# Wider VectorE operations, a 16-bit softmax and a re-cut start in a fused attention and GEGLU block on one Trainium2 core

## The chip, the cores and the metric

The kernel runs on one core of one Trainium2 chip. The metric is the device time of one execution in microseconds; a kernel's time is the median of several runs. Beside the runs there is one profiled execution, whose trace gives each instruction's start and length. Times inside an execution are counted from the start of the profile's span.

## What is computed

Input x has 2048 rows of 512 bf16 values. It is layer-normalised, and from the normalised rows two branches are computed and added to x itself.

```python
def _A_ref(x, wqkv, wo):                 # 32 heads of 16, window W = 8, dilation 2
    q, k, v = ...                        # x @ wqkv, split by head
    idx = pos[:, None] - off[None, :]    # each row looks at rows s, s-2, ..., s-14
    logits = einsum("bhsd,bhswd->bhsw", q, kg) * scale    # -1e9 where idx < 0
    o = einsum("bhsw,bhswd->bhsd", softmax(logits), vg)
    return o @ wo

def _B_ref(x, w_gate, w_up, w_down):     # 512 -> 1376 -> 512
    h = gelu(x @ w_gate) * (x @ w_up)
    return h @ w_down

xn = _layernorm(x)
return x + _A_ref(xn, A_wqkv, A_wo) + _B_ref(xn, B_w_gate, B_w_up, B_w_down)
```

## The kernel before

**Blocks and tiles.** The 2048 rows are worked in four blocks (b = 0 to 3) of 512 rows, each of four tiles of 128 rows. Within a block the data lie transposed: features on the partitions, rows along the free dimension (`xnT`).

**Normalisation.** Two tiles share one buffer `XIN` (four buffers, 128x2x512 bf16). Tiles 0 to 7 are normalised on VectorE (statistics L750 and L776, subtraction L861, multiplication by the reciprocal root L873); tile 1 has part of its statistics on ACT (L752 to L766). Tiles 8 to 15 are normalised on ACT (L769, L815, L846, L853), with the root on GpSimd (L832). Block 0's tiles are transposed by TensorE through an identity matrix (L899) and copied out of PSUM (L911 on VectorE, L919 on ACT); those of blocks 1 to 3 by DMA transposes (L882), issued by SP.

**Projections.** In block 0, Q and K are computed tile by tile with matmuls of 128 columns (`mmt`, L959); the first tile's first quarter is a group of its own (`mma0_0`). V of block 0 and all of Q, K and V in blocks 1 to 3 come in four groups g of four matmuls with 512 columns each (L1009). ACT copies every group out of PSUM (L986, L1020). Group g holds four of the sixteen values of each head, for all 32 heads and 512 rows.

**Attention.** For each group g, VectorE multiplies Q by eight shifted views of K in one operation of 4096 elements a partition (`pr`, L1040), written in fp16 to one of six `UNI` buffers. Pairs of products are added (`pa`, L1053), which leaves two sums; in block 3 (`PR_ADD3 = (3,)`) a third add makes them one. TensorE sums over the partitions that belong to one head by matmuls with the small matrix `E8` (group `er`, L1085): 8 for each remaining sum, so 16 in blocks 0 to 2 and 8 in block 3. The same group first computes the last 64 columns of the up projection (L1078, 16 matmuls of 256 columns).

The logits lie in two PSUM banks, for 128 partitions and 8 window positions by 128. The softmax works on them there: in block 0 a mask is added (L1111), then VectorE takes the maximum over the window (`d1`, L1117, a reduction) and subtracts it (`d2`, L1122), both on fp32 in PSUM. ACT takes the exponential into fp16 (`exp`, L1133), VectorE sums the eight positions by three halving adds (`d4a` to `d4c`, L1141), ACT makes the reciprocal as exp(-ln) (`ln` L1151, `d5` L1155), and VectorE multiplies (`d6`, L1159) into `PB`. Four DMAs store `PB` to a scratch tensor in HBM (`ss`, L1169) and four load it back, repeated over the partitions, into `PT` (`sl`, L1180).

VectorE then multiplies V's shifted views by `PT`, two window positions at a time (`pv`, L1188, 4096 elements), adds the four products (`pw`, three adds of 4096, L1197) and the two halves (`pz`, 2048, L1203) into `OT`.

**Feed-forward and output.** Gate and up projections run in 11 column groups j, of four matmuls with 512 columns each (`fg` and `fu`, L1221; the last gate group L1260). ACT applies gelu (L1231) and copies the up part (L1238), VectorE multiplies both (`h`, L1245) into `HT`. For each tile t, a group `acc` (L1306) accumulates `OT` times Wo and `HT` times Wd in one PSUM bank. In blocks 0 to 2 the Wo part comes first (in `acca` or `accd`); in block 3 it comes last (`accw`), and the last two tiles are cut into column parts. ACT copies the result out (`fe`, L1339), VectorE adds the tile's rows of x, which were loaded again into one of two `XR` buffers (`ldxr`, L1292; the add `fin`, L1344, or straight from PSUM, L1350), and SP stores them (`sto`, L1357).

**What sets the order.** Every operation is a task of a graph. `ORDER` (L404 to L461) is the order of all tasks on each of the five engines, written out by name. Each engine works in this order, waits on semaphores for what a task reads and for the buffers that it reuses, and never passes a waiting task. `schedule` (L207) only decides which buffer of a pool a task gets and thereby which earlier user it waits for; its duration constants (`PARAMS`, `SCHED`, `d_mm`, `d_dve`, `d_act`) issue nothing. PSUM is one pool of eight banks. All DMAs are issued by SP: x's first tiles and Wq, Wk, Wv first, then x2, x4, x3, Wg (which waits until Wk has landed), Wu and the rest. An issue takes 0.4 to 0.7 us of SP, a transpose about 1.3.

**The start.** TensorE runs 15 matmuls on constants first (L678), with the first transpose among them. In the order before, `mma0_0` is followed by the second tile's transpose, the Q and K groups of tiles 0 to 3, two groups of V (`mm0_2_2`, `mm0_2_1`), the first Wg group (`fg0_0`), a third group of V, three Wg groups, two Wu groups and the fourth group of V.

Of the kernel before, what the change touches and what calls it, by code (L numbers as in the profile page):

```python
# [6 lines left out]
ENGS = ("pe", "act", "dve", "pool", "sp")  # L7

PARAMS = dict(
    LAT_X=0.08,  # L10
    LAT_S=0.03,
    TOL=dict(pe=0.6, act=-0.3, dve=0.0, pool=0.0, sp=0.0),
    DMA_ISSUE=0.48,
    DMA_FIXED=2.0,
    DMA_BPUS=330e3,
    ACT_SWITCH=1.35,
    PE_SLACK=0.0,
    PE_MODE_SWITCH=0.115,
    PE_DRAIN=0.2,
    DRAIN=0.1,  # L20
    PE_COLD_F=2.0,
    HAM_TAU=4.0,
    HAM_ENTER=0.52,
    HAM_EXIT=0.30,
)


class PeClock:

    def __init__(self, prm):  # L30
        self.tau = prm["HAM_TAU"]
        self.enter = prm["HAM_ENTER"]
        self.exit = prm["HAM_EXIT"]
        self.f = prm["PE_COLD_F"]
        self.avg = 0.0
        self.t = 0.0
        self.warm = False

    def run(self, start, dur, util):
        import math  # L40
        if start > self.t:
            self.avg *= math.exp(-(start - self.t) / self.tau)
            if self.warm and self.avg < self.exit:
                self.warm = False
            self.t = start
        left = dur
        total = 0.0
        while left > 1e-9:
            step = min(left, 0.2)
            real = step * (1.0 if self.warm else self.f)  # L50
            a = math.exp(-real / self.tau)
            self.avg = self.avg * a + util * (1.0 - a)
            if not self.warm and self.avg > self.enter:
                self.warm = True
            elif self.warm and self.avg < self.exit:
                self.warm = False
            total += real
            left -= step
        self.t = start + total
        return total  # L60

# [36 lines left out]
class Task:  # L98
    def __init__(self, idx, eng, name, dur, emit, prio, table, nbytes, batch, mode=None, latest=None,
# [6 lines left out]
        self.on_act = False  # L106
        self.idx = idx
# [28 lines left out]
class Graph:  # L136
# [70 lines left out]
    def schedule(self, orders, params=None):  # L207
        prm = dict(PARAMS)
        prm.update(params or {})
        LAT_X, LAT_S = prm["LAT_X"], prm["LAT_S"]  # L210
# [12 lines left out]
        efree = dict((e, 0.0) for e in ENGS)  # L223
        act_table = None
        pe_mode = None
        pe_clock = PeClock(prm)
        dma_free = 0.0

        def rdy(t, p, od):
            if p.eng == t.eng and (p.eng == "pe" or od):  # L230
                return p.end
            return p.done + (LAT_S if p.eng == t.eng else LAT_X)

# [33 lines left out]
        for _ in range(len(self.tasks)):  # L267
# [17 lines left out]
            if t.eng == "sp":  # L285
                t.end = est + (t.dur or prm["DMA_ISSUE"])
                t.done = t.end
                if t.nbytes > 0:
                    dma_free = max(t.end, dma_free) + t.nbytes / prm["DMA_BPUS"]
                    t.done = dma_free + prm["DMA_FIXED"]  # L290
            elif t.eng == "pe":
# [5 lines left out]
                t.end = est + sw + pe_clock.run(est, t.dur, t.util)  # L297
                t.done = t.end + prm["PE_DRAIN"]
            else:
                t.end = est + t.dur  # L300
                t.done = t.end + prm["DRAIN"]
# [87 lines left out]
    def report(self):  # L389
# [16 lines left out]
        "warm0 warm1 warm2 warm3 warm4 warm5 warm6 warm7 warm8 warm9 tpx0_0 warm10 warm11 warm12 warm13 "  # L406
        "warm14 mma0_0 tpx0_1 mmt0_0 mmt0_1 mmt1_0 tpx1_0 mmt1_1 mmt0_2 tpx1_1 mmt1_2 mmt0_3 mmt1_3 "
        "mm0_2_2_0 mm0_2_1_0 fg0_0 mm0_2_0_0 fg0_1 fg0_2 fg0_3 fu0_0 fu0_1 mm0_2_3_0 fg0_4 fu0_2 fu0_3 fu0_4 "
        "fg0_5 mm1_1_0_0 mm1_0_0_0 fu0_5 fg0_6 er0_3 mm1_0_1_0 mm1_1_1_0 fg0_7 mm1_1_3_0 mm1_0_2_0 mm1_2_3_0 "
        "fg1_0 mm1_0_3_0 mm1_1_2_0 fg1_1 fu1_0 fu1_1 fu0_6 fu0_7 fg1_2 fu1_2 mm1_2_2_0 mm1_2_1_0 fg1_3 fu1_3 "  # L410
        "fg0_8 fg1_4 fu0_8 mm1_2_0_0 fg1_5 fg0_9 fu1_4 fu0_9 fu1_5 fg1_6 fg0_10 fu1_6 mm2_0_0_0 mm2_1_0_0 "
        "mm2_1_1_0 mm2_0_2_0 er1_3 fg1_7 mm2_0_3_0 mm2_0_1_0 fg1_8 mm2_1_3_0 mm2_2_0_0 fg2_0 mm2_1_2_0 accd2 "
        "fu1_7 accd1 mm2_2_2_0 fu1_8 acca0 fg1_10 mm2_2_3_0 accb0 fg2_1 fg2_2 accd3 fg2_3 fu2_0 fg1_9 fu2_1 "
        "mm2_2_1_0 fu2_2 fu2_3 er2_3 mm3_1_0_0 mm3_1_3_0 fu1_9 mm3_0_0_0 mm3_1_2_0 mm3_0_2_0 mm3_2_1_0 "
        "mm3_0_1_0 mm3_1_1_0 fg3_0 mm3_0_3_0 fg2_4 mm3_2_0_0 mm3_2_2_0 mm3_2_3_0 fu3_0 fu2_4 fg2_5 fg2_10 "
        "accd7 fu2_5 fg3_1 fu3_1 fg3_2 accd5 acca4 er3_3 fg2_6 accb4 accd6 fu2_6 fg2_7 fg2_8 fg3_10 fu2_7 "
        "fu3_2 fu2_8 fg3_3 fg3_4 fu3_3 fg3_5 fg2_9 fu2_9 fu3_4 fg3_6 fu3_5 fg3_7 fu3_6 fu3_7 fg3_8 fg3_9 "
        "fu3_8 accd11 acca8 accd10 fu3_9 accd9 accb8 acca12 accd13 accd14_0 accd14_1 accw14_0 accw14_1 "
        "accw13 accd15_0 accb12 accw15_0 accw12 accd15_1 accw15_1 accd15_2 accw15_2",
    "act":  # L420
        "c_tbl sx1 sq0 negm1 sxx1 sq1 evx0_0 evx0_1 evq0_0 sq2 evq0_1 evk0_0 evx1_0 sq3 evk0_1 bnst8 evx1_1 "
        "bnst9 evq0_2 evk0_2 evq0_3 evk0_3 ve8 sq6 vp8 sq4 bnag8 evv0_2_0 evv0_1_0 halo1 bnag9 evv0_0_0 va8 "
        "gelu0_0 bnst10 gelu0_2 uev0_0 bnst11 ve10 evv0_3_0 gelu0_1 vp10 gelu0_3 uev0_3 uev0_1 bnag10 "
        "evk1_0_0 evq1_0_0 gelu0_5 bnag11 gelu0_4 uev0_5 uev0_4 uev0_2 vb8 evq1_1_0 evk1_1_0 gelu0_6 gelu0_7 "
        "exp0 sub8 va10 evq1_2_0 vb10 ln0 sub11 d5_0 evk1_3_0 evq1_3_0 evv1_3_0 uev1_0 evk1_2_0 sub9 uev1_1 "
        "uev0_6 uev0_7 gelu1_1 gelu1_0 evv1_1_0 sub10 norm9 uev0_10b gelu1_3 evv1_2_0 gelu0_8 norm10 norm8 "
        "uev1_2 gelu1_2 norm11 gelu1_5 uev1_3 gelu1_4 bnst12 gelu0_9 uev0_9 uev1_5 uev0_8 uev0_10a bnst13 "
        "uev1_6 uev0_10c evv1_0_0 evq2_0_0 gelu0_10 evk2_1_0 ve12 evk2_0_0 vp12 evq2_2_0 bnag12 gelu1_6 "
        "uev1_4 evq2_3_0 gelu1_7 bnag13 evq2_1_0 halo2 evk2_3_0 exp1 bnst14 va12 bnst15 vb12 ve14 evk2_2_0 "
        "vp14 uev1_10b bnag14 ln1 uev1_7 d5_1 sub13 halv1 fe2 bnag15 uev1_8 va14 vb14 sub15 sub12 fe1 "  # L430
        "uev1_10c evv2_2_0 sub14 norm12 norm13 fe0 evv2_3_0 evv2_0_0 gelu2_2 gelu2_1 norm14 fe3 norm15 halo3 "
        "uev1_10a gelu2_0 gelu1_10 uev2_1 evv2_1_0 uev2_0 uev2_3 uev2_2 gelu1_8 uev2_10b uev2_10c gelu2_3 "
        "gelu1_9 evq3_0_0 evk3_0_0 evq3_2_0 evk3_3_0 evk3_2_0 evq3_1_0 exp2 halv2 evk3_1_0 uev1_9 evv3_0_0 "
        "evv3_3_0 ln2 evv3_2_0 evq3_3_0 d5_2 evv3_1_0 uev3_0 halv3 gelu2_5 uev2_10a gelu2_4 uev2_5 uev2_4 "
        "uev3_1 fe5 gelu2_10 gelu3_1 fe7 fe4 uev3_10c gelu3_2 gelu3_0 exp3 uev3_10b uev2_6 uev2_7 fe6 ln3 "
        "uev3_2 d5_3 uev2_8 gelu2_6 uev3_3 gelu2_7 gelu2_9 uev2_9 gelu2_8 gelu3_4 gelu3_5 uev3_5 gelu3_3 "
        "gelu3_6 uev3_6 uev3_4 uev3_7 gelu3_7 fe11 gelu3_10 fe10 gelu3_9 uev3_10a uev3_9 gelu3_8 uev3_8 fe8 "
        "fe9 fe13 fe12",
    "dve":
# [25 lines left out]
def d_mm(n, cnt=1):  # L465
    return cnt * max(64, n) * 0.4213e-3


def d_act(n):
    return 0.10 + 0.00085 * n  # L470
# [950 lines left out]
```

## Time and profile before

| what | value |
|---|---|
| median of 3 runs | 184.14 us (184.11 to 184.27) |
| profiled execution, span | 182.8 us |
| granted TensorE clock | 0.999 of full speed |
| TensorE / VectorE / ACT busy | 178.0 / 168.8 / 129.3 us |
| DMA, mean over the span | 107 GB/s, 19.60 MB |
| first 17.17 us: VectorE / ACT busy, DMA | 11.2 / 12.6 us, 304 GB/s |
| 17.17 to 77 us: TensorE / VectorE / ACT busy | 59.8 / 59.4 / 54.9 us of 59.8 |
| 77 to 137 us: TensorE / VectorE / ACT busy | 60.0 / 59.3 / 43.4 us of 60.0 |
| 137 to 180.3 us: TensorE / VectorE / ACT busy | 43.3 / 38.6 / 18.4 us of 43.3 |

The median of the runs is 1.3 us above the span of the profiled execution; what lies outside the span is not in the trace. A group's line gives the code line, engine, operation, operands with their shape, the count, then busy time in us and the mean length of one in ns, then the idle time of the engine just before it. The lengths of neighbouring VectorE operations overlap by some 85 ns, so the distance from one start to the next is less than the length. In the chain of waits each row is a stretch of the chain that ended last: its start, its length, and the engine and line, or the DMA, that it belongs to.

### The profile page before, as it was taken

What the parts mean: (1) busy time and instruction counts of PE and PEld (TensorE: products, weight loads), DVE (VectorE), ACT (ScalarE), POOL (GpSimd) and SP (SyncE); (2) the same over time, 40 slices, a digit from 0 to 9 for tenths busy, and PEclk for the clock granted to TensorE, in tenths of its full rate; (3) what the DMA queues carried; (4) which work ended last, traced back from release to release, by engine and by line L of the source; (5) the groups of instructions that cost most, each with busy time, mean ns of one, the idle gap of its engine ahead of it and who ended that gap; (6) DMA issues with size and microseconds to landing.
All of it is one profiled execution on the core that took longest, in us unless ns stands there. A gap on an engine that the chain in (4) does not pass through costs nothing.

```text
span 182.8 us, 2777 instructions
## 1 busy us (share of the span) xinstructions
PE 178.0 (97%) x1060; PEld 89.8 (49%) x1060; DVE 168.8 (92%) x169; ACT 129.3 (71%) x266; POOL 11.1 (6%) x23
## 2 busy tenths in 40 slices
PE   8799999999999999999999999999999999999994
PEld 2685444554444544444444555444444444444673
DVE  3769999999999999999999989999999999999932
ACT  5589977899899899869997596934396764145011
POOL 6000000104000000504000000000000000000000
PEclk9999999999999999999999999999999999999999
DMA  4999559610364000002742000136310246222333
GB/s 111 359 376 377 132 113 299 211 50 21 97 190 98 0 0 0 4 14 74 201 115 61 0 0 0 37 81 158 129 59 0 46 138 221 57 84 74 91 106 107
DMA packets 26220, 19.60 MB, mean 107 GB/s; under 512 B 13824, under 2 KB 23008, under 8 KB 26208
## 3 DMA queue, kind: packets, MB, share of 16 engines
q1 hardware_dynamic: 26208, 19.44, 36.3%
q8 instruction: 8, 0.13, 0.3%
q14 instruction: 4, 0.03, 0.1%
HBM read 14.71 MB, written 3.15 MB: 98 GB/s over the span
## 4 chain that ended last, share of the span: by engine, by line
PE 89%; DMA 8%; SPq 1%; issue 0%; DVE 0%; DVEq 0%
PE PS L1221 38%; PE PS L1306 28%; PE PS L1009 18%; DMA Wg<-in_B_w_gate_dram 5%; DMA Wqkv<-in_A_wqkv_dram 3%; PE PS L1260 2%; PE PS L1085 2%; PE PS L1078 1%; SPq L731 1%; SPq L687 0%; DVE OB L1350 0%; DVEq L376 0%
## 5 line engine op out<-in xcount | busy, mean ns | idle before, releaser
L1306 PE MATMUL PS<-Wd,HT 128*128 128x512 bf16 (+2 forms) x209 | 40.8, 345 | 0.0
L1221 PE MATMUL PS<-xnT,Wg 128*128 128x512 bf16 x160 | 39.6, 379 | 0.3 <-DMA Wg<-in_B_w_gate_dram 0.3
L1221 PE MATMUL PS<-xnT,Wu 128*128 128x512 bf16 x160 | 38.8, 379 | 0.0
L1009 PE MATMUL PS<-xnT,Wqkv 128*128 128x512 bf16 x160 | 37.8, 379 | 0.0
L1040 DVE TENSOR_TENSOR UNI<-QT,KT 128x4096 f16<-128x4096 bf16 x16 | 36.4, 2287 | 0.1
L1188 DVE TENSOR_TENSOR UNI<-VN,PT 128x4096 f16<-128x4096 bf16 x16 | 36.0, 2286 | 0.0
L1306 PEld LDWEIGHTS PS<-Wd,HT 128*128 128x128 bf16 x209 | 19.7, 98 | 19.0
L1238 ACT ACTIVATE UU<-PS 128x512 bf16<-128x512 f32 x40 | 22.8, 604 | 7.9 <-PE PS L1221 6.2
L1197 DVE TENSOR_TENSOR UNI<-UNI 128x4096 f16<-128x4096 f16 x12 | 27.4, 2286 | 0.0
L1009 PEld LDWEIGHTS PS<-xnT,Wqkv 128*128 128x128 bf16 x160 | 17.9, 114 | 16.9 <-ACT UU L1238 0.4
L1231 ACT ACTIVATE GG<-PS 128x512 bf16<-128x512 f32 x40 | 23.4, 600 | 2.5 <-DVE HT L1245 1.7
L1221 PEld LDWEIGHTS PS<-xnT,Wg 128*128 128x128 bf16 x160 | 15.4, 98 | 19.6 <-DMA Wg<-in_B_w_gate_dram 0.7
L1221 PEld LDWEIGHTS PS<-xnT,Wu 128*128 128x128 bf16 x160 | 15.7, 98 | 18.8
L1339 ACT ACTIVATE OB<-PS 128x512 bf16<-128x512 f32 x14 | 8.2, 594 | 21.8 <-PE PS L1306 21.8
L1053 DVE TENSOR_TENSOR UNI<-UNI 128x4096 f16<-128x4096 f16 x9 | 20.4, 2282 | 0.0
L1306 PE MATMUL PS<-Wo,OT 128*128 128x512 bf16 (+2 forms) x76 | 16.5, 345 | 0.0
L1245 DVE TENSOR_TENSOR HT<-GG,UU 128x1024 bf16<-128x1024 bf16 x20 | 13.6, 686 | 0.0
L832 POOL TENSOR_TENSOR sq<-ve,mhalf 128x2 bf16<-128x2 f32 x4 | 8.2, 2058 | 73.3 <-ACT ve L828 73.3
L1020 ACT ACTIVATE VN<-PS 128x512 bf16<-128x512 f32 x16 | 9.3, 594 | 2.5 <-PE PS L1009 2.5
L1306 PEld LDWEIGHTS PS<-Wo,OT 128*128 128x128 bf16 x76 | 7.2, 98 | 6.5
L1020 ACT ACTIVATE QT<-PS 128x512 bf16<-128x512 f32 x12 | 7.2, 597 | 3.2 <-PE PS L1009 3.2
L959 PE MATMUL PS<-xnT,Wqkv 128*128 128x128 bf16 x128 | 8.2, 219 | 1.2 <-DMA Wqkv<-in_A_wqkv_dram 1.0
(85 smaller groups left out, 153.9 us busy)
## 6 DMA issues: line engine op xcount, KB each, us to landing
PT<-pt_scratch SPq DMA_DIRECT2D x16, 256.0 KB, 4.0
XR<-in_A_x_dram SPq DMA_DIRECT2D x16, 128.0 KB, 2.4
out_dram<-OB SPq DMA_DIRECT2D x14, 128.0 KB, 2.0
Wqkv<-in_A_wqkv_dram SPq DMA_DIRECT2D x3, 512.0 KB, 5.6
XIN<-in_A_x_dram SPq DMA_DIRECT2D x6, 256.0 KB, 6.0
Wg<-in_B_w_gate_dram SPq DMA_DIRECT2D x1, 1280.0 KB, 8.8
Wu<-in_B_w_up_dram SPq DMA_DIRECT2D x1, 1280.0 KB, 11.6
Wd<-in_B_w_down_dram SPq DMA_DIRECT2D x1, 1280.0 KB, 7.7
```

The lines of the kernel that those rows point to most:

```text
L832: "pool", "sq%d" % t, 7.0, lambda e, t=t, n=n: e.tensor_tensor(out=sq[:, t:t + n], in0=ve[:, t:t + n], in1=mhalf[:, 0:n], op=ALU.pow),
L1009: ins = e.matmul(PS[:, 512 * it.slot:512 * it.slot + 512], lhsT=wcols(which, kt, g), rhs=xnT[:, itx.slot, kt, :], start=(kt == 0), stop=(k ...
L1020: return e.activation(out=o, in_=PS[:, 512 * it.slot:512 * it.slot + 512], func=ACTF.Identity, scale=(QSC, 1.0, 1.0)[which])
L1040: return lambda e: e.tensor_tensor(out=UNI[:, it.slot, :, :], in0=bass.AP(QT, (itq.slot * 4 + g) * 512, [[NQT * 4 * 512, 128], [0, 8], [1, ...
L1053: return lambda e: e.tensor_tensor(out=UNI[:, i0.slot, :, :], in0=UNI[:, i0.slot, :, :], in1=UNI[:, i1.slot, :, :], op=ALU.add)
L1188: return lambda e: e.tensor_tensor(out=bass.AP(UNI, ito.slot * 4096, [[NUNI * 4096, 128], [2048, 2], [512, 4], [1, 512]]), in0=bass.AP(VN, ...
L1197: return lambda e: e.tensor_tensor(out=UNI[:, i0.slot, :, :], in0=UNI[:, i0.slot, :, :], in1=UNI[:, i1.slot, :, :], op=ALU.add)
L1221: ins = e.matmul(PS[0:M, 512 * it.slot:512 * it.slot + 512], lhsT=Wx[:, kt, j * 128:j * 128 + M], rhs=xnT[:, itx.slot, kt, :], start=(kt = ...
L1231: return lambda e: e.activation(out=GG[:, ito.slot, q, :], in_=PS[:, 512 * it.slot:512 * it.slot + 512], func=ACTF.Gelu_apprx_tanh)
L1238: return lambda e: e.activation(out=UU[:, ito.slot, q, :], in_=PS[:, 512 * it.slot:512 * it.slot + 512], func=ACTF.Identity)
L1245: return lambda e: e.tensor_tensor(out=HT[:, ito.slot, j - 1:j + 1, :], in0=GG[:, ig.slot, :, :], in1=UU[:, iu.slot, :, :], op=ALU.mult)
L1306: ins = e.matmul(PS[:, 512 * it.slot:512 * it.slot + CW], lhsT=(OT[:, ito.slot, q, ti * 128:(ti + 1) * 128] if kind == "o" else HT[:, ith. ...
```

## The change

- **VectorE, wider**: `pr` is one operation for two groups (8192 elements, two a block in place of four); `pa` adds both pairs at once (8192); `pv` takes four window positions (8192, two a block); `pw` is one add of 8192 and one of 4096. Buffers of `UNI` and `PT` are taken in pairs.
- **Third add**: a further add of 4096 (`pb`) folds the two sums into one in blocks 1, 2 and 3 (`PR_ADD3 = (1, 2, 3)`; block 3 had it). `er` has 8 matmuls on `UNI` in these blocks.
- **Softmax in 16 bits**: ACT copies the logits from PSUM to `PB` in bf16 (`lc`, 1024 elements). VectorE takes the maximum by three halving operations (`d1a`, `d1b`, `d1c`: 512, 256, 128) in a bf16 view of `SU` and subtracts in place in `PB` (`d2`, 1024); `exp` reads `PB`.
- **The start**: Wq is loaded by two DMAs, rows 0 to 255 and 256 to 511. For tiles 0 and 1, the multiplication of the normalisation, the transpose and the Q group are each cut in two halves of the features (`norm0a`/`norm0b`, `tpx`/`tpy`, `mma`/`mmb`). V of block 0 is computed in four groups of 8 matmuls with 256 columns, each for half of the rows and two of the four g (`mmv`).
- **Residual rows**: those of blocks 2 and 3 (`ldxr8` to `ldxr15`) are loaded into `XIN` buffers, two tiles in each; those of blocks 0 and 1 stay in `XR`.
- **Orders**: `ORDER` is rewritten for all engines but GpSimd. The first Wg group comes after three groups of V (`mmv0_1`, `mmv0_0`, `mmv1_0`); the fourth (`mmv1_1`) comes after `fg1_4`. In SP's order x5 comes before the small parts of Wt, and the transposes of tiles 4 to 7 before Wt's last two parts. `schedule` has other duration constants; the simulated clock of TensorE is gone.

The core of the diff:

```diff
+            if i == 0:
+                for h in range(2):
+                    def mk(h=h):
+                        return lambda e: e.dma_start(
+                            Wqkv[:, 2 * h:2 * h + 2, 0:512],
+                            A_wqkv[256 * h:256 * h + 256, 0:512].rearrange("(k p) n -> p k n", p=128))
...
-    PR_ADD3 = cfg.get("PR_ADD3", (3,))
+    PR_ADD3 = cfg.get("PR_ADD3", (1, 2, 3))
...
+                        def mk_mv(h=h, gp=gp, it=it_mm, itx=XTI[0]):
...
+                                        ins = e.matmul(PS[:, c:c + 256], lhsT=wcols(2, kt, 2 * gp + g),
+                                                       rhs=xnT[:, itx.slot, kt, 256 * h:256 * h + 256],
+                                                       start=(kt == 0), stop=(kt == 3))
...
+            for h in range(2):
+                def mk_p(h=h, it=pr_items[h], itq=it_qt, itk=KTI[b]):
+                    return lambda e: e.tensor_tensor(
+                        out=UNI[:, it.slot:it.slot + 2, :, :],
+                        in0=bass.AP(QT, (itq.slot * 4 + 2 * h) * 512, [[NQT * 4 * 512, 128], [512, 2], [0, 8], [1, 512]]),
+                        in1=bass.AP(KT, (itk.slot * 4 + 2 * h) * 528 + 2,
+                                    [[2 * 4 * 528, 128], [528, 2], [2, 8], [1, 512]]),
+                        op=ALU.mult)
...
+            if b in PR_ADD3:
+                def mk_pb(i0):
+                    return lambda e: e.tensor_tensor(
+                        out=UNI[:, i0.slot, :, :], in0=UNI[:, i0.slot, :, :], in1=UNI[:, i0.slot + 1, :, :], op=ALU.add)
...
-                return lambda e: e.tensor_reduce(
-                    out=msv(0), in_=lgv(0, 128, [(1, 128), (128, 8)]), axis=AX.X, op=ALU.max)
+                return lambda e: e.activation(out=PB[:, it.slot, :], in_=lgv(0, 128, [(1, 1024)]), func=ACTF.Identity)
+            for k, w in enumerate((512, 256, 128)):
+                def mk_d1(w=w, it=it_pb):
+                    return lambda e: e.tensor_tensor(
+                        out=SUB[:, 0:w], in0=PB[:, it.slot, 0:w] if w == 512 else SUB[:, 0:w],
+                        in1=PB[:, it.slot, w:2 * w] if w == 512 else SUB[:, w:2 * w], op=ALU.max)
...
+                    in1=bass.AP(SUB, 0, [[512, 128], [0, 8], [1, 128]]), op=ALU.subtract)
...
-                    return e.activation(out=EX[:, :], in_=lgv(0, 128, [(1, 1024)]), func=ACTF.Exp)
+                    return e.activation(out=EX[:, :], in_=PB[:, it.slot, :], func=ACTF.Exp)
```

The order on VectorE from the first wide product to block 0's sum, and around it, in the changed kernel:

```
pr0_1 pr0_0 pa0 h0_1 mask h0_0 rstd8 d1a_0 d1b_0 d1c_0 d2_0 pr1_0 d4a_0 rstd10 d4b_0 d4c_0 h0_2 d6_0 pr1_1
h1_0 pa1 h0_10 pb1 h0_3 pv0_1 d1a_1 h1_1 h0_4 d1b_1 pv0_0 d1c_1 h1_2 d2_1 h1_3 pw0_1 d4a_1 pw0_2 d4b_1 pz0
```

Around block 2's sum (`pz2`) it is `pw2_1 pw2_2 h3_2 pz2 fin5`, and around block 3's `pv3_1 pw3_1 fin9 pw3_2 pz3`. TensorE's first use of them is `accd3` for pz0, `acca8` for pz2 and `accw13` for pz3.

## The prediction

> **What bounds the kernel now.** I read the page's busy time and its 40 slices first, then the chain of waits, then the groups by line with shapes kept apart (for prices), then the timeline of the last 12 us.
>
> ```profile
> PE 178.0 (97%) x1060; PEld 89.8 (49%) x1060; DVE 168.8 (92%) x169; ACT 129.3 (71%) x266; POOL 11.1 (6%) x23
> PE   8799999999999999999999999999999999999994
> DVE  3769999999999999999999989999999999999932
> ACT  5589977899899899869997596934396764145011
> ```
>
> TensorE and VectorE are both full; ACT is full only until about 60 us.
>
> ```profile
> 2.75 5.60 DMA Wqkv<-in_A_wqkv_dram
> 8.37 8.76 DMA Wg<-in_B_w_gate_dram
> 17.17 1.04 PE PS L1221 x4
> 18.21 0.86 PE PS L1009 x4
> ...
> 32.02 0.55 PE PS L1078 x16
> 32.58 0.86 PE PS L1085 x16
> ...
> 128.78 0.55 PE PS L1078 x16
> 129.33 0.43 PE PS L1085 x8
> ...
> 163.53 16.75 PE PS L1306 x122
> ```
>
> The columns are start, length, what. From 17.17 us, when Wg lands, to 180.28 us the chain is TensorE work and nothing else: 163.1 us without a wait. So the end moves by what leaves or enters this stretch, plus any wait that appears in it. Ahead of it the chain is loads.
>
> ```profile
> 172.12 1.22 DVE L1203 TENSOR_TENSOR OT<-UNI 128x2048 bf16<-128x2048 f16 x1
> ...
> 173.76 1.04 PE L1306 MATMUL PS<-Wo,OT 128*128 128x256 bf16 x8
> ```
>
> VectorE's last attention sum ends at 173.34 us, 0.42 us before TensorE uses it. VectorE is no wait now, but has nothing to spare: it is the second bound.
>
> **Prices (groups by line).**
>
> ```profile
> L1040 DVE TENSOR_TENSOR UNI<-QT,KT 128x4096 f16<-128x4096 bf16 x16 | 36.4, 2287 | 0.1
> L1122 DVE TENSOR_TENSOR PS<-PS,ms 128x1024 f32<-128x1024 f32 x4 | 4.9, 1228 | 0.0
> L1117 DVE TENSOR_REDUCE ms<-PS 128x128 f32<-128x1024 f32 x4 | 4.9, 1222 | 0.0
> L1133 ACT ACTIVATE EX<-PS 128x1024 f16<-128x1024 f32 x4 | 4.1, 1023 | 0.0
> L1159 DVE TENSOR_TENSOR PB<-EX,rc 128x1024 bf16<-128x1024 f16 x4 | 2.7, 685 | 0.0
> ```
>
> [...] 1228 and 1222 ns in PSUM against 685 in SBUF for 1024 elements. [...] The trace: 1221 ns for 2048 elements and 2287 for 4096 give 0.52 ns an element and 155 ns fixed, of which neighbours overlap 85 (the timeline shows 2.20 us from start to start), so a merged pair saves only 0.07 us. [...] L1133 has 1.02.
>
> **The change, part by part.**
>
> 1. *Third adds in blocks 1 and 2* (block 3 has its own already). TensorE's group er makes 8 instead of 16 matmuls on UNI: 0.43 us by L1085 (0.86 for 16), twice: −0.86 us, wholly on the path. VectorE gets two adds of 4096 (pb): 2 x 2.20 = +4.4 us.
>
> 2. *The front.* Block 0's V projection is cut in halves of rows, 8 matmuls of 256 columns each; the split tails show 11 such in 1.20 us, so 0.87 us a group. Before, two of V's four groups (0.86 each) ran ahead of Wg and two behind. Now three are ahead, one behind: −0.86 us on the path, if they fit. Wg's time stays: the same bytes stand ahead of it in the queue, which moves about 360 GB/s from 4.6 us on, so 17.1. TensorE's first real matmul, now at 6.65, waits for all of Wq (landed 6.51, x's next 128 KB 0.38 us later). At that rate the first 256 KB land 0.75 us sooner, 5.76; normalised x is there at about 5.7 (now 5.87: half of a 351 ns norm less). Work to do before 17.17: 16 transposes and 128 matmuls of 56 ns (8.1 us) and three V groups (2.6 us), 10.7 us from 5.85, plus some 0.4 us of waiting for Wk (landed 8.35): done near 16.9. It fits by 0.3 us. Wq's second DMA puts 0.47 us of SP issue ahead of x's tiles 2 and 3, Wk, Wv and x2; these are issued by 5.1 us and land at 6.9 to 11.2 behind a backlog, so I take nothing, at most 0.2. Wu landed 3.28 us after Wg and is now needed after four Wg groups, 3.45 us: free by 0.2.
>
> 3. *Softmax in 16 bits.* Out: reduction and PSUM subtraction, 2 x 1.14 us from start to start. In: three maxima (512, 256, 128: 0.335, 0.20, 0.135) and a subtraction like L1159, 0.60: 1.27 us. That is −1.0 us of VectorE a block. [...] ACT gets a copy (lc) of 1.02 us a block. It frees two PSUM banks some 6 us sooner; no TensorE wait is there to be removed by that.
>
> 4. *Wide ops.* 22 pairs merged: −1.5 us of VectorE. A wide op costs between 4.33 us (taken) and two of 2.20; [...] the V product already has three free dimensions and runs at 2286 ns.
>
> 5. *Late residual rows in x's buffers.* Today's adds wait 1.1 us in all for these rows, off the path; 0. Halved norms: +0.15 us each on VectorE, before the full stretch.
>
> VectorE in sum: +4.4 − 4.0 − 1.5 = −1.1 us, before waits. The new order adds waits in block 0. The mask comes one 0.6 us op after the add that er needs; er takes 1.70 us to it (31.86 to 33.56 today). The maximum stands one op after the mask and needs lc's 1.1 us; the last multiplication stands one op after the sums and needs two ACT steps. I get 1.5, 0.5 and 0.6: 2.6 us, where the trace has 0.3. x's tiles 4 to 7 are normalised ahead of the wide product instead of around it, which starts at 16.65. From there, at the durations above, VectorE needs 133.0 us of work to the end of block 2's sum (pz2), so 152.2; TensorE wants it 26.2 us before its end, at 152.4. Block 0's pz0 comes at 75.1, wanted at 75.1; block 3's pz3 at 172.5, wanted at 173.2. So VectorE is just in time at three places and any lateness of it goes to the end one to one.
>
> Sum: last matmul 180.28 − 0.86 − 0.86 = 178.56; span 182.80 − 1.72 = 181.08. The runs' median of 184.14 lies 1.34 above the profiled execution's span; I keep that: 182.42. With 0.1 us for small waits, **182.5**.
>
> **Queues that steps are moved past.** Transposes of x's tiles 4 to 7 (1.3 us of SP issue each) now stand in front of Wt's last parts and behind x5; TensorE needs them at 24.9, I get 23 to 24. In block 0, one of x's transposes stands between the loads of PT, needed 5 us later. In block 1 lc stands in front of two norms on ACT; their transposes land near 62.3, wanted at 63.7.
>
> **The rivals.**
>
> *The front doesn't fit*: V's third group reaches past Wg, up to 0.87 us lost: 183.3. For it: only 0.3 us of room and two waits in the way. Against it: the trace has 0.4 us of idle before Wg with two groups, and starts 0.8 us later. 8%.
>
> *VectorE takes over the bound, within the gain*: waits or maxima cost 0.5 to 1.5 us more than my ledger: 182.9 to 183.9, about 183.3. For it: three just-in-time places[...]. Against it: the written orders put wide ops over every other hand-over in blocks 1 to 3. 22%.
>
> *Slower*: the waits of block 0's softmax. ACT works in order and is 92% busy there (54.9 of 59.8 us to 77 us); lc, exp and ln of block 0 stand behind one to five evacuations that themselves follow TensorE. Each that comes late adds 0.5 us to a wait that VectorE can't fill. From 4.7 us of waits (2.6 + 2.1) on the kernel is slower than before; with 5.2 us it takes 185.0. 9%.
>
> *The work before Wg shortens the loads too* (ramp of the queue at 3 to 4.5 us): 0.3 to 0.5 us less, 182.0. 5%.
>
> The first case has the remaining 56%: 182.1 to 182.9. Below about 182.0 I leave 4%; above 183.8, what is left of the VectorE case and the slower one, 13%: range 182.0 to 183.8. What a measurement here can tell from no change is about 0.2%, 0.37 us: faster means under 183.77, slower over 184.51. Faster: 56 + 8 + 19 + 5 and less 4 for steps that I overlooked, 0.84; same 0.07; slower 0.09.
>
> **What would show it.** er of blocks 1 and 2 with 8 matmuls on UNI and 0.43 us each; Wg's first matmul at 17.1 to 17.3 after 24 of V's matmuls; wide products at 4.4 us; 685 ns subtractions; TensorE without a wait but for some tenths; waits of 1.5, 0.5 and 0.6 us on VectorE in block 0; pz2 within 0.3 us of its use. Wrong would be: a Wg matmul after 17.5, TensorE waiting on OT for over half a microsecond, or waits on ACT in the stretch from 20 to 60 us.

## The result, and the profile after

| kernel | median, us | runs | ratio to the kernel before, 95% interval |
|---|---|---|---|
| before | 184.14 (183.93 to 184.42) | 12 | |
| changed | 183.84 (183.24 to 185.19) | 12 | 0.999 (0.9975 to 1.0006) |
| changed, second series | 183.93 (183.62 to 184.62) | 22 | 0.9989 (0.9976 to 1.0002) |

The forecast was 182.5. The change is worth 0.2 to 0.3 us where 1.7 was expected, and both intervals take in no change at all. The changed kernel's profiled execution took 184.79 us, with a span of 182.7.

First the page of the changed kernel: busy times and slices.

```profile
PE 177.2 (97%) x1060; PEld 90.5 (50%) x1060; DVE 169.0 (92%) x157; ACT 131.8 (72%) x270; POOL 17.4 (10%) x23
PE   7799999999999999999999999999999999999994
DVE  3779997699999999989999999999999999999953
ACT  5569989999999999999387598844268679411030
POOL 6000006200000000974000000000000000000000
```

TensorE's work fell by 0.8 us and VectorE's hardly moved, though in 12 instructions fewer. New is GpSimd, at 17.4 us instead of 11.1. Next the chain of waits (start, length, what).

```profile
3.21 6.05 DMA Wqkv<-in_A_wqkv_dram
9.26 0.02 issue
9.27 8.87 DMA Wg<-in_B_w_gate_dram
18.14 0.05 issue
18.19 7.94 PE PS L1259 x36
...
72.70 8.31 POOL sq L803
81.01 0.02 issue
81.03 0.17 DVE rstd L774
...
91.98 0.17 DVE rstd L774
92.15 0.02 issue
92.17 1.33 ACT XIN L824 x2
93.51 0.48 ACT VN L1050
93.99 0.98 ACT UU L1276 x2
94.97 0.14 issue
95.11 0.62 PE PS L1106 x16
95.73 0.43 PE PS L1113 x8
...
154.12 0.04 issue
154.16 26.20 PE PS L1351 x165
```

Before, this chain was loads and then TensorE alone. Now Wg starts it 1.0 us later (18.19 for 17.17), and it leaves TensorE for a long detour: GpSimd's root of tile 12, VectorE's reciprocals of the roots of tiles 12 and 14 (`rstd12`, `rstd14`, L774, 0.16 us each; the expectations below call them copies), the norms of tiles 15 and 12 on ACT, three PSUM copies, and only then block 2's group `er` at 95.11. The groups that answer to the prices:

```profile
L1221 DVE TENSOR_TENSOR UNI<-VN,PT 128x8192 f16<-128x8192 bf16 x8 | 35.4, 4420 | 0.0
L1070 DVE TENSOR_TENSOR UNI<-QT,KT 128x8192 f16<-128x8192 bf16 x8 | 35.3, 4419 | 0.0
L1142 ACT ACTIVATE PB<-PS 128x1024 bf16<-128x1024 f32 x4 | 4.1, 1032 | 3.8 <-PE PS L1113 3.7
L1147 DVE TENSOR_TENSOR SU<-PB 128x512 bf16<-128x512 bf16 x4 | 1.7, 420 | 0.4 <-ACT PB L1142 0.4
L803 POOL TENSOR_TENSOR sq<-ve,mhalf 128x2 bf16<-128x2 f32 x4 | 14.6, 3642 | 68.3 <-ACT ve L799 68.3
```

Every price of the forecast is there; the last row is the one it did not have.

**The sum.** I cut the execution at Wg's first matmul and at the end of the last one, and call what lies between the dense stretch. Without waits the changed stretch would be 163.1 less 0.86 for the V group moved ahead of it and less 0.86 for the third adds: 161.4 us.

| kernel | Wg's first matmul | dense stretch | last matmul |
|---|---|---|---|
| before | 17.17 | 163.1 | 180.3 |
| forecast | 17.2 | 161.4 | 178.6 |
| changed | 18.19 | 162.15 | 180.3 |
| changed, second series | 17.50 | 162.16 | 179.7 |

(In four of the experiments' traces the first record of the stretch is missing; the distance to the later groups `er` puts it 0.22 us ahead of the first one recorded, and I use that.) The 1.72 us of TensorE work are gone. But the stretch has 0.75 us of TensorE waits that it did not have (each is the extra distance from one matmul's start to the next; the idle time that a view shows is up to 0.16 us less): 0.25 at 49.4 us before a projection of block 1 (ACT's PSUM copy), 0.29 at 95.1 us before block 2's `er`, 0.21 at 154.1 us before the first use of block 2's last attention sum `pz2`. And it starts 0.5 to 1.0 us later.

### The profile page after: what moved, and what is told of

Read it like the earlier page. It is cut to its first block, busy times and chain, and to the rows that moved or that the text cites. A ratio compares the mean times of both kernels' runs of the same rounds, so it can differ in the third digit from the quotient of the medians.

```text
span 182.7 us, 2780 instructions
## 1 busy us (share of the span) xinstructions
PE 177.2 (97%) x1060; PEld 90.5 (50%) x1060; DVE 169.0 (92%) x157; ACT 131.8 (72%) x270; POOL 17.4 (10%) x23
## 4 chain that ended last, share of the span: by engine, by line
PE 55%; ACT 22%; DMA 8%; DVE 6%; POOL 5%; issue 2%; SPq 1%; DVEq 0%
PE PS L1351 23%; PE PS L1259 21%; PE PS L1039 9%; DMA Wg<-in_B_w_gate_dram 5%; POOL sq L803 5%; ACT UU L1276 4%; ACT GG L1269 4%; DMA Wqkv<-in_A_wqkv_dram 3%; DVE UNI L1070 2%; ACT XIN L824 2%; DVE UNI L1082 2%; ACT L1164 1%; ACT EX L1165 1%; ACT PB L1142 1%; ACT KT L1050 1%
## 5 line engine op out<-in xcount | busy, mean ns | idle before, releaser
L1259 PE MATMUL PS<-xnT,Wu 128*128 128x512 bf16 x160 | 39.4, 379 | 0.0
L1221 DVE TENSOR_TENSOR UNI<-VN,PT 128x8192 f16<-128x8192 bf16 x8 | 35.4, 4420 | 0.0
L1070 DVE TENSOR_TENSOR UNI<-QT,KT 128x8192 f16<-128x8192 bf16 x8 | 35.3, 4419 | 0.0
L1039 PE MATMUL PS<-xnT,Wqkv 128*128 128x512 bf16 x144 | 34.7, 379 | 0.1
L1039 PEld LDWEIGHTS PS<-xnT,Wqkv 128*128 128x128 bf16 x144 | 16.2, 114 | 15.6 <-ACT UT L1314 0.6
L803 POOL TENSOR_TENSOR sq<-ve,mhalf 128x2 bf16<-128x2 f32 x4 | 14.6, 3642 | 68.3 <-ACT ve L799 68.3
L1082 DVE TENSOR_TENSOR UNI<-UNI 128x8192 f16<-128x8192 f16 x4 | 17.7, 4420 | 0.0
L1230 DVE TENSOR_TENSOR UNI<-UNI 128x8192 f16<-128x8192 f16 x4 | 17.7, 4420 | 0.0
L1236 DVE TENSOR_TENSOR UNI<-UNI 128x4096 f16<-128x4096 f16 x4 | 9.1, 2286 | 0.0
L1050 ACT ACTIVATE KT<-PS 128x512 bf16<-128x512 f32 x12 | 7.2, 601 | 2.0 <-PE PS L1039 2.0
L1050 ACT ACTIVATE VN<-PS 128x512 bf16<-128x512 f32 x12 | 7.2, 597 | 1.0 <-PE PS L1039 0.9
```

Source lines behind the costliest of these rows:

```text
L803: "pool", "sq%d" % t, 5.0, lambda e, t=t, n=n: e.tensor_tensor(out=sq[:, t:t + n], in0=ve[:, t:t + n], in1=mhalf[:, 0:n], op=ALU.pow),
L1039: ins = e.matmul(PS[:, 512 * it.slot:512 * it.slot + 512], lhsT=wcols(which, kt, g), rhs=xnT[:, itx.slot, kt, :], start=(kt == 0), stop=(k ...
L1050: return e.activation(out=o, in_=PS[:, 512 * it.slot:512 * it.slot + 512], func=ACTF.Identity, scale=(QSC, 1.0, 1.0)[which])
L1070: return lambda e: e.tensor_tensor(out=UNI[:, it.slot:it.slot + 2, :, :], in0=bass.AP(QT, (itq.slot * 4 + 2 * h) * 512, [[NQT * 4 * 512, 1 ...
L1082: return lambda e: e.tensor_tensor(out=UNI[:, i0.slot:i0.slot + 2, :, :], in0=UNI[:, i0.slot:i0.slot + 2, :, :], in1=UNI[:, i1.slot:i1.slo ...
L1221: return lambda e: e.tensor_tensor(out=bass.AP(UNI, ito.slot * 4096, [[NUNI * 4096, 128], [2048, 4], [512, 4], [1, 512]]), in0=bass.AP(VN, ...
```

## The experiments

**Both kernels again.** `e0_before` and `e1_after_again` are the two kernels unedited.

> The kernel before, profiled once more. Its first profile has Wk landing at 8.35 us, Wg at 17.13, the last matmul ending at 180.3, span 182.8. If the start is steady (theory: the new start itself costs the 1.0 us by which Wg came later in the changed kernel), Wk lands again within 0.2 us of 8.35 and Wg within 0.3 of 17.1. If the landing of the loads differs from execution to execution (rival: chance), Wg lies anywhere between 16.5 and 18.2 and the spans of its runs differ by as much. It also shows how a run's time stands to its span: 1.3 us above it if the first profile was a median run, 2.1 as in the changed kernel if it was a slow one.

> The changed kernel, profiled once more; 183.8 us and runs between 183.2 and 185.2 as before. Theory GpSimd (wide VectorE operations keep GpSimd from its root operation): the four roots take anything from 1 to 9 us, tile 12's differs from the 8.3 us of the first profile by over 2 us, and VectorE's wait of 0.58 us for it comes and goes with it. Theory loads: Wk lands near 9.3 and Wg near 18.1 again. Rival chance: Wk and Wg land near 8.4 and 17.1 this time, and the span is then near 181.7.

Before: 184.14 (ratio 0.9999, 0.9984 to 1.0015). Changed: 183.93. Spans lie 1.8 to 2.1 us under the times in the kernel before (1.95 in the mean of 59 executions) and 2.0 to 2.2 in the changed one (2.10, 22 executions). So the kernel before's first profiled execution, with a span of 182.8, took an estimated 184.7 and was some 0.6 us slower than its median. In the second series' traces Wg's first matmul is at 16.96 (before) and 17.50 (changed); the waits in the stretch are the same to 0.02 us.

**GpSimd's root.** In `e2_root_on_vector` VectorE takes the roots of tiles 8 to 15, in `e3_ops_split` every operation of 8192 elements is two of 4096.

```diff
-  "pool", "sq%d" % t, ... e.tensor_tensor(out=sq[:, t:t + n], in0=ve[:, t:t + n], in1=mhalf[:, 0:n], op=ALU.pow)
+  "dve", "sq%d" % t, ... e.tensor_scalar(out=sq[:, t:t + n], in0=ve[:, t:t + n], scalar1=1.25, scalar2=0.2,
+                                         op0=ALU.mult, op1=ALU.add)
...
-  return lambda e: e.tensor_tensor(out=UNI[:, i0.slot:i0.slot + 2, :, :], ...)       # e3, here pa; pr, pv, pw alike
+  for r in range(2):
+      ins = e.tensor_tensor(out=UNI[:, i0.slot + r, :, :], ...)
```

> The changed kernel with the roots of tiles 8 to 15 taken off GpSimd: VectorE computes them as 1.25 v + 0.2, the tangent of the root at a variance of 0.16, four instructions of 0.15 us. Theory GpSimd: VectorE's wait of 0.58 us and TensorE's of 0.35 us before er of block 2 go, so 183.2 to 183.5, and the runs lie within 0.6 us of each other as those of the kernel before do. Rivals loads and ACT: the same 183.6 to 184.0 with the same spread of 2 us.

> The changed kernel with each operation of 8192 elements (pr, pa, pv, pw) issued as two of 4096, same order. VectorE gets 22 times 0.07 us more, 1.5 us. Theory GpSimd: the roots take 0.7 to 2.7 us again as in the kernel before, VectorE doesn't wait for tile 12's, but being later by 1.0 us at block 2's sum, TensorE waits there: 184.4 to 185. If width costs nothing but those 0.07 us (rival), the roots take as long as in the changed kernel and the time is 184.6 to 185.2.

Root on VectorE: 183.73 (183.03 to 184.21, ratio 0.9974, 0.9962 to 0.9986); VectorE's 0.58 us wait is gone, the stretch takes 161.91, and block 2's `er` is where the 0.24 us went. (The interval of the ratio overlaps the changed kernel's; the stretch is the firmer evidence.) Split: 184.32 (ratio 1.0014, 0.9998 to 1.0029), and tile 12's root still took 8.58 us. So it is not the width of the operations. Its other reading is the price of VectorE's time: it was busy for 170.5 us instead of 169.0, and the time rose by only 0.4. But the dense stretch took 163.20 us, 1.05 more, and TensorE's longer waits stand at the same two places:

```profile
94.30 0.62 PE L1114 MATMUL PS<-xnT,Wt 128*32 128x256 bf16 x16 [0.64 <-ACT UU L1292]
153.96 1.04 PE L1367 MATMUL PS<-Wo,OT 128*128 128x512 bf16 x4 [0.52 <-DVE OT L1257]
```

Inside the stretch 1.5 us of VectorE therefore cost 1.05. The time hides it: in this kernel all 14 executions lie only 1.7 us above their spans, 0.37 less than in the changed kernel, and why is open. My next theory was that GpSimd gets no turn as long as VectorE runs operations with two SBUF inputs back to back. The timeline of VectorE in the changed kernel, beside tile 12's root on GpSimd (72.70 to 81.00):

```profile
74.50 0.28 DVE L1173 TENSOR_TENSOR SU<-SU 128x256 f16<-128x256 f16 x1
74.70 1.22 DVE L1241 TENSOR_TENSOR OT<-UNI 128x2048 bf16<-128x2048 f16 x1
75.83 0.28 DVE L1173 TENSOR_TENSOR ms<-SU 128x128 f32<-128x128 f16 x1
76.04 4.42 DVE L1070 TENSOR_TENSOR UNI<-QT,KT 128x8192 f16<-128x8192 bf16 x1
81.03 0.17 DVE L774 RECIPROCAL rstd<-sq 128x2 f32<-128x2 bf16 x1 [0.58 <-POOL sq L803]
```

Each operation starts before the one ahead of it has ended, until VectorE itself stops for the root at 80.45; 0.55 us later the root is done. `e7_rstd12_later` moves `rstd12`, and with it the stop.

```diff
-  ... d4c_1 pr2_0 rstd12 d6_1 pr2_1 h1_10 fin3 h1_4 pa2 ...
+  ... d4c_1 pr2_0 d6_1 pr2_1 h1_10 rstd12 fin3 h1_4 pa2 ...
```

> The changed kernel with one short VectorE step moved: the copy of tile 12's root, for which VectorE waited 0.6 us on GpSimd, stands three products and a multiplication later (about 7 us). If GpSimd's root is merely slow (8.3 us) or late, it is done long before, the wait goes, block 2's group on TensorE comes 0.2 to 0.3 us sooner, and the time is 183.7. If the root is held off for as long as VectorE runs operations with two SBUF inputs one after the other without a gap, it ends about 0.5 us after VectorE stops, wherever the copy stands: the root then lasts 8 to 15 us, and a wait of 0.3 to 0.6 us stays in front of the moved copy unless another wait of VectorE lets the root through first.

183.96 (ratio 0.9996, 0.9983 to 1.0008). The root's row in this run (durations in ns: least, median, most) and who waited for it:

```profile
L803 POOL TENSOR_TENSOR sq<-ve,mhalf x4: 687/2128/13563, 26.7 to 85.4; 128x2 bf16<-128x2 f32 x4
  DVE rstd L774: 0.6, 1
```

The same operation on 128x2 values took 13.6 us, and the 0.58 us wait moved along with `rstd12`. So this root was not slow in itself: it was held off until VectorE stopped. But my theory, that it gets no turn in an unbroken run of VectorE operations, is too strong. Tile 14's root in the changed kernel, with the VectorE operation beside it:

```profile
81.70 4.42 DVE L1070 TENSOR_TENSOR UNI<-QT,KT 128x8192 f16<-128x8192 bf16 x1
84.66 2.01 POOL L803 TENSOR_TENSOR sq<-ve,mhalf 128x2 bf16<-128x2 f32 x1 [3.66 <-ACT ve L799]
```

It ended at 86.67, 0.55 us after that operation, although VectorE's next one had begun at 86.04. In `e6_no_third_add` and `e9_f32_softmax`, below, tile 12's root got its turn in the same way, 0.55 us after the first VectorE operation that ended beside it (2.37 and 2.57 us), where the changed kernel's was passed over four times. So the roots that took over 1.2 us all end 0.55 to 0.57 us after the end of some VectorE operation; at which one is open. A root of 0.71 us in the kernel before, at 34.33, began and ended beside a VectorE reduction from PSUM (L1117, 33.88 to 35.11). Nor does the order of starting tell: four VectorE operations that started after tile 12's root at 72.70, from 74.50 to 76.04, went ahead of it. What holds a root off is not shown.

**The start.** `e4_wq_whole` loads Wq by one DMA; `e5_wg_no_wait` drops the rule that Wg is issued after Wk has landed; `e10_before_split` cuts Wq's DMA in two in the kernel before and changes nothing else.

```diff
-  "ld_x0_0 ld_x0_1 ld_wq0 ld_wq1 ld_x1_0 ld_wk ..."          # e4; e10 has it the other way round
+  "ld_x0_0 ld_x0_1 ld_wq0 ld_x1_0 ld_wk ..."
...
-  t_w.deps.add(t_ld["wk"])                                   # e5
```

> The changed kernel with Wq loaded by one DMA again; nothing else is moved. If the second DMA of Wq is what delays Wk (landed at 8.4 to 9.3 us in four profiled executions of the changed kernel and its variants, at 8.32 and 8.35 in the kernel before), Wk lands at 8.3 to 8.4 here, the first V product leaves TensorE about 8.45 us later, Wg's first matmul starts at 17.0 or at Wg's landing, and the time is 0.3 to 0.6 us under the changed kernel: about 183.5. If the queue's landings vary by themselves, Wk stays between 8.4 and 9.3 and the time at 183.9. If the early start on half of Wq was worth something, it gets slower: 184.2.

> The changed kernel without the rule that SyncE issues Wg only after Wk has landed. The theory that Wg's landing sets the start of the dense stretch: the queue's dip at 10.5 to 12 us goes, Wg lands 0.4 to 0.8 us sooner (16.0 to 16.8), and the time falls by as much, to 183.4. The theory that Wk's landing plus 8.45 us of TensorE work sets it: Wg lands sooner, but the first Wg matmul stays at Wk plus 8.45, and the time within 0.2 of 183.9; if Wg's bytes then compete with those of Wk and x, the start is even later.

> The kernel before with one edit: Wq is loaded by two DMAs of half its rows each; every consumer waits for both. If the second DMA is what spreads and delays the landings behind it, Wk lands at 8.4 to 9.3 us instead of 8.32 and 8.35, Wg, issued after Wk, at 17.0 to 18.1 instead of 16.9 and 17.1, and the time is 0.1 to 0.6 us over the kernel before: 184.2 to 184.7. If the later landings of the changed kernel have another cause, such as the transposes or the order of loads, it stays at 184.1.

Whole Wq: 183.46 (183.15 to 183.92, ratio 0.9964, 0.995 to 0.9978), 0.47 us under the changed kernel, with Wg's first matmul at 16.79 and the same 162.15 us of stretch. The kernel before with halves: 184.61 (184.28 to 185.24, ratio 1.0036, 1.0022 to 1.005). Two kernels, one edit in opposite directions, 0.5 us each: the second DMA costs that. In the traces of the changed kernel and its variants Wg's first matmul comes at 16.9 to 18.2 with halves (mean 17.4, eight traces) and at 16.65 to 17.1 with a whole Wq (mean 16.9, six). The one trace of `e10_before_split` does not show its loss: its first Wg matmul, at 17.06, lies between the two of the unedited kernel. No wait for Wk: 183.99 (ratio 0.9997); Wg landed at 17.51, no sooner, so that rule costs nothing.

What goes with the cost is seen in the landings. Over the nine traces with halves the last of the 16 DMA engines brings its part of Wk at 8.2 to 9.3 us, mean 8.73; over the eight with a whole Wq at 7.6 to 8.35, mean 8.0. The first engine brings it at 6.8 to 7.3 in all of them. With halves the engines lie further apart, and a consumer waits for the last: in the first trace of the changed kernel Wk's parts came at 7.13 to 9.26 us, and TensorE's first K group, after 1.17 us of waiting, started at 9.30. Wg lands at 17.06 in the mean for 16.72. Why the halves spread them is open. What TensorE makes of it is in the chain of `e4_wq_whole`:

```profile
6.08 0.61 PE PS L965 x8
...
8.39 0.89 PE PS L951 x16
...
15.10 1.75 PE PS L1009 x16
16.85 0.16 issue
17.01 7.72 PE PS L1254 x35
```

From 6.08 to 16.85 the chain is TensorE without a gap, 10.8 us, of which 8.46 from the first K group on. With Wk at 9.00, as in the second series, these 8.46 us end at 17.46, and Wg, there since 16.51, waits for TensorE. In the first trace of the changed kernel it was the other way round: TensorE's part would have ended at 17.7, and Wg landed at 18.14.

**The third adds and the softmax.** `e6_no_third_add` leaves out the third adds of blocks 1 and 2; `e9_f32_softmax` has the old softmax in PSUM, with block 2's exponential three places earlier in ACT's order.

```diff
-    PR_ADD3 = cfg.get("PR_ADD3", (1, 2, 3))                  # e6; and pb1, pb2 out of VectorE's order
+    PR_ADD3 = cfg.get("PR_ADD3", (3,))
...
-  e.activation(out=PB[:, it.slot, :], in_=lgv(0, 128, [(1, 1024)]), func=ACTF.Identity)      # e9
-  e.tensor_tensor(out=SUB[:, 0:w], ..., op=ALU.max)                 # w = 512, 256, 128
+  e.tensor_reduce(out=ms2[:, :], in_=lgv(0, 128, [(1, 128), (128, 8)]), axis=AX.X, op=ALU.max)
```

> The changed kernel with the third adds of blocks 1 and 2 left out, so that TensorE sums two UNI buffers there (16 matmuls, 0.86 us, instead of 8, 0.43); all else as changed. If the adds gain what they save on TensorE (0.86 us) less the waits that they bring (0.2 to 0.4 us at block 2's group, which comes late behind VectorE, and 0.2 at the last sum of block 2), the time is 0.3 to 0.6 us over the changed kernel: 184.2 to 184.5. If VectorE, which is freed of 4.4 us, was the bound, it does not get slower, or gets faster: 183.9 or less.

> The changed kernel with the softmax of before: maximum by reduction and subtraction in PSUM, no copy on ScalarE (block 2's exponential moves three places up in ScalarE's order so that PSUM suffices); all else as changed. VectorE then has about 1.0 us more a block, 3 us up to block 2's last sum and 4 in all. If every microsecond of VectorE goes to the end, as the prediction held at its three just-in-time places, the time is 186 to 187. If only part does, as when the merged operations were undone (1.5 us more work cost 0.45), it is 184.5 to 185.3. If ScalarE's copy costs as much as VectorE saves, it is within 0.3 of 183.9.

Without third adds: 184.18 (ratio 1.0004, 0.9991 to 1.0018), 0.25 us over the changed kernel. The stretch takes 162.52, 0.37 more, where 0.86 us of TensorE work came back: the waits at block 2's `er` and at `pz2`, 0.50 us, were gone. So the two adds are worth 0.4 and not 0.86 us. That VectorE's 4.4 us took the rest is not shown cleanly: in this run tile 12's root took 2.37 us and VectorE did not wait for it, so GpSimd's part of the waits went too.

The old softmax: 189.98 (189.78 to 191.51, ratio 1.0352), beyond all that was expected. VectorE was busy 172.7 us, 3.7 more, 0.93 a block, as priced. But the time went elsewhere, as the waits show:

```profile
PEld PS L1040 <- ACT EX L1158: 3.6, 3, 3.0
PE PS L1040 <- ACT EX L1158: 2.5, 1, 2.5
```

The longest of TensorE's waits is in block 2, where a projection waits for PSUM banks until ACT's exponential has read the logits. The other three long ones, 0.7 to 1.1 us each, are for other PSUM copies by ACT. In the new order the copy `lc` is what frees the logits' banks in time (in the changed kernel TensorE's weight loads wait 0.2 and 0.3 us for it, its matmuls not at all). The run does not tell what a microsecond of VectorE is worth here, which is what it was for.

**Order.** Are the three waits mere order, or is VectorE the bound behind them? `e8_orders` had whole Wq and three moves:

```diff
-  VectorE: ... pa2 fin0 rstd14 pb2 pv1_0 ...    +  ... pa2 pb2 fin0 rstd14 pv1_0 ...
-  VectorE: ... pw2_2 h3_2 pz2 fin5 ...          +  ... pw2_2 pz2 h3_2 fin5 ...
-  TensorE: ... fg1_3 mm1_2_2_0 fu1_3 ...        +  ... fg1_3 fu1_3 mm1_2_2_0 ...
```

> The changed kernel with Wq loaded by one DMA and three places in the written orders altered: block 2's third add stands ahead of two short VectorE steps instead of behind them, block 2's last attention sum ahead of one FFN product, and on TensorE one projection of block 1 changes places with the FFN group behind it. If the three waits of TensorE in the dense stretch (0.25, 0.29 and 0.2 us) are mere order, they go, the stretch takes 161.4 to 161.5 us instead of 162.15, and with the earlier start (16.8) the time is 182.7 to 182.9. If VectorE or ScalarE is the bound behind them, the waits come back at the next hand-over and the time stays at 183.3 to 183.5, what the whole Wq alone gave.

186.4 (185.26 to 187.64, ratio 1.0129): slower. The third move had given 47 TensorE groups other PSUM banks, so `e11_two_orders` made only the first two, with the banks as before.

> The changed kernel with Wq loaded by one DMA and two places in VectorE's written order altered: block 2's third add ahead of two short steps instead of behind them, and block 2's last attention sum ahead of one FFN product. TensorE's order and its PSUM banks stay as in the changed kernel (the exchange on TensorE, which altered the banks of 47 groups, is left out). If the two waits on VectorE (0.29 us at block 2's group, 0.2 us at the output projection of block 2) are order alone, they go, the dense stretch takes 161.65 to 161.75 us instead of 162.15, and the time is 182.9 to 183.1. If the third add comes no sooner because VectorE is behind as a whole, or another hand-over waits in their place, it is 183.4 to 183.5, what the whole Wq alone gave; if these two edits and not the banks made the altered orders slow, it is 185 to 186.5.

187.13 (185.28 to 187.4, ratio 1.0157): it was not the banks. ACT and TensorE in `e11_two_orders`:

```profile
93.04 1.33 ACT L819 ACTIVATE XIN<-XIN,rstd 128x512 bf16<-128x512 bf16 x2 [3.94 <-DVE rstd L769]
95.88 0.62 PE L1101 MATMUL PS<-xnT,Wt 128*32 128x256 bf16 x16 [2.44 <-ACT UU L1271]
```

I had taken block 2's `er` to wait for the third add. It waits for ACT, which stands behind a norm that needs `rstd14`, and my move had put that 0.16 us step behind the 2.2 us add. (The runs fall at 185.3 and at 187.1 to 187.4; the profile is one of the former, and the further 1.8 us of the latter are in no trace.) The chain of the changed kernel had said so from the start. `e12_rstd14_sooner` therefore moves only that step, the other way; `e13_three_orders` adds two moves.

```diff
-  VectorE: ... h1_4 pa2 fin0 rstd14 pb2 ...     +  ... h1_4 rstd14 pa2 fin0 pb2 ...         # e12, e13
-  VectorE: ... pw2_2 h3_2 pz2 fin5 ...          +  ... pw2_2 pz2 h3_2 fin5 ...              # e13
-  ACT: ... ve12 uev0_10a uev0_10b uev0_7 ...    +  ... uev0_10a uev0_10b ve12 uev0_7 ...    # e13
```

> The changed kernel with Wq loaded by one DMA and one short VectorE step moved: the copy of tile 14's root (0.16 us), for which ScalarE waits 1.6 us in the trace, stands ahead of block 2's wide sum instead of behind it and behind one output addition, some 4.8 us sooner; the third add keeps its place but for these 0.1 us. If block 2's group on TensorE is late because ScalarE's evacuations stand behind that copy, it comes 0.29 us sooner, the stretch takes 161.85 us instead of 162.15, and the time is 183.1 to 183.3, against 183.46 for the whole Wq alone. If it is late because of the third add on VectorE, the group stays late and the time is 183.4 to 183.5.

With one move: 183.25 (183.08 to 183.52, ratio 0.9946, 0.9933 to 0.9958). `er` came 0.28 us sooner, counted from Wg's first matmul, so it was ACT behind `rstd14`. But the stretch stayed at 162.14: what was won at `er` was lost at `pz2`, where the wait grew from 0.21 to 0.48. The time is 0.2 under that of the whole Wq alone, but the two intervals overlap.

> The same with two more moves: block 2's last attention sum ahead of one FFN product on VectorE, and in block 1 a 0.2 us step of ScalarE for tile 12 behind two PSUM copies instead of between them (TensorE waits 0.25 us for the second). PSUM banks are those of the changed kernel. If the three waits are order alone, the stretch takes 161.4 to 161.5 us, the saved 1.72 us of TensorE are all there, and the time is 182.7 to 182.9. If VectorE or ScalarE bounds behind them, other waits take their place and it is 183.1 or more.

With three: 183.05 (182.82 to 183.35, ratio 0.993, 0.9917 to 0.9943). The stretch is 161.88. The wait before block 1's projection is down to 0.09 and that at `pz2` to 0.05. The largest one left, 0.29 us, is new and stands at block 3's last sum, `pz3`, as the chain of this run shows:

```profile
169.92 2.21 DVE UNI L1231
172.13 0.02 issue
172.15 1.24 DVE OT L1236
173.39 0.05 issue
173.44 5.49 PE PS L1346 x50
```

TensorE's first use of `pz3` is at 173.44. So what is left is VectorE, and its lateness has moved on to the next place where it is just in time (the expectation that follows still speaks of `pz2`). `e14_orders_and_root` gives it back its 0.58 us wait, by the root on VectorE as in `e2_root_on_vector`.

> The kernel with whole Wq and three altered orders, and the roots of tiles 8 to 15 not taken by GpSimd's power but by VectorE's tangent 1.25 v + 0.2 of the root at variance 0.16 (an approximation: part of the computation is changed). VectorE no longer waits 0.58 us for GpSimd and has four short steps more (0.1 us each). If that wait was what made block 2's last attention sum late, TensorE's 0.35 us wait there goes, the stretch takes 161.4 to 161.55 us, and the time is 182.6 to 182.8. If VectorE is behind for other reasons (its waits in block 0), the stretch stays at 161.8 to 161.9 and the time at 183.0.

182.73 (182.55 to 183.38, ratio 0.9937, 0.9924 to 0.995), the stretch 161.60, 0.08 at `pz3`. With the start repaired, three steps moved and VectorE's wait gone, the time is within 0.25 us of the forecast. `e13_three_orders`, which alters orders and one load alone, beats both kernels; what `e14_orders_and_root` adds rests on the approximated root. It shows in the stretch, by 0.28 us, and not in the ratio: the kernel before took 184.00 beside this run and 184.23 beside `e13_three_orders`.

## Why the prediction was wrong

From 182.42 to the 183.9 measured are 1.5 us. Two terms failed, both put at next to nothing: TensorE's waits in the stretch ("some tenths", 0.1 us in the sum, where 0.75 came) and Wq's second DMA ("I take nothing", where 0.5 came). The remaining 0.2 us I can't place: it is as large as the differences of single executions at the start.

1. *Third adds, −0.86 on TensorE.* Right: 8 matmuls and 0.43 us in blocks 1 to 3. Their price on VectorE, 4.4 us, was right too, but with the waits they are worth 0.37 us of stretch and not 0.86 (`e6_no_third_add`).
2. *"Wq's second DMA ... I take nothing, at most 0.2", and "Wg's time stays: the same bytes stand ahead of it".* Here the forecast failed first. I reasoned from bytes and from SP's issue time. The bytes were the same, but Wk's last part came 0.7 us later in the mean, and the second DMA costs 0.5 us. The work on TensorE ahead of Wg was right: 10.7 us forecast, 10.8 measured. It does fit when Wq is whole. Of the forecast's own signs of being wrong, "a Wg matmul after 17.5" came, at 18.19.
3. *Softmax.* VectorE's saving of 1.0 us a block measured 0.93 (`e9_f32_softmax`); `lc` took 1.03 us, forecast 1.02; the first maximum 420 ns against a price of 335 from start to start, which is the same after the overlap of 85 (the price was an estimate, from the adds of L1141 and their 423 ns). In block 0, where the three maxima and the subtraction stand next to each other, each waits for the one before and nothing overlaps (each starts 0.03 us after that one's end): 1.65 us in the trace for 1.27 in the forecast. "It frees two PSUM banks some 6 us sooner; no TensorE wait is there to be removed by that" was right of the old order only: the new one needs the banks.
4. *Wide operations.* 4.42 us each, 4.34 from start to start, forecast 4.33; undone, they cost VectorE 1.5 us, as forecast, the stretch 1.05 and the time 0.4.
5. *Late rows.* No wait on them in the trace.

*VectorE's waits in block 0*: forecast 1.5, 0.5 and 0.6 us, measured 1.8, 0.4 and 0.25; these held. The sum did not: VectorE's work was to fall by 1.1 us and its busy time rose by 0.2. In the second series the wide product starts at 16.66, as forecast (16.65), and `pz0` ends at 75.23 for 75.1, but `pz2` at 153.42 for 152.2. Of these 1.2 us 0.58 are the wait for GpSimd, which the ledger lacked; the rest is open. The forecast had not looked at GpSimd's four roots, whose busy time rose from 8.2 to 14.6 us. *"VectorE is just in time at three places"* was the most useful sentence in it. `pz2` came at 154.10, TensorE used it at 154.16 and 0.21 us late. "Any lateness of it goes to the end one to one" was nearly right inside the stretch: there 1.5 us more of VectorE cost 1.05 (`e3_ops_split`), and with TensorE's other waits gone the lateness came out at `pz3` (`e13_three_orders`).

*The rivals.* "The front doesn't fit" and "VectorE takes over the bound, within the gain" both came, each for half of the loss and each by a cause that I had not named: landings spread by one more DMA, and GpSimd with ACT behind it. I had priced them as alternatives, at 183.3 each; together they end at 183.9. *The 1.34 us outside the span* was mis-sized: it is about 1.95. The kernel before's profiled execution was slow by the difference, and by luck the two errors cancel.

## What to carry to other kernels

When an engine has no slack left, price every wait that it hands on, GpSimd's included: a 0.2 us step in VectorE's order that another engine waits for counted for more here than the 2.2 us add beside it (with the add moved ahead of the step TensorE waited 2.44 us at `er`; with the step moved ahead `er` came 0.28 us sooner). Cutting a load in two at the head of the DMA queue moved the last landings of the loads behind it, with the same bytes (Wk's by 0.7 us in the mean). Read what an edit costs from the stretch too, not from the time alone. And add up rivals that can come together, before giving each a chance of its own.

## What the runs showed of the hardware

- GpSimd's power on 128x2 values took from 0.69 to 13.6 us. The longer ones, beside VectorE operations with two SBUF inputs, ended about 0.55 us after one of these ended: mostly the first, often without a stop of VectorE (tile 14's, 2.01 us), but tile 12's root, in most runs of the changed kernel's kind, only when VectorE stopped, with operations of 4096 elements (8.6 us) as of 8192 (8.3 us). What decides which end lets it through was not tried.
- One more DMA of 256 KB, with no more bytes, put the last of 16 engines' part of a load that was issued two DMAs later 0.7 us back in the mean (8.73 us in nine traces, for 8.0 in eight), the first engine's part not at all (6.8 to 7.3 us in all of them).
